# Holding the plan to late landings: a self-scheduling attention and SwiGLU kernel with new landing floors, fill products and load order

## The chip, the cores and the metric

The kernel runs on one core of one Trainium2 chip. The metric is the device time of that core in microseconds (us). The kernel before took 438.62 us, the median of five runs (436.72, 437.76, 438.62, 439.91 and 439.95). The profiled execution is the fastest of the five.

## The reference

The inputs are q, k and v of shape 8 x 12 x 448 x 64 (batch, heads, sequence, head width), two FFN weights of 768 x 1536, an output weight of 1536 x 768 and a norm gain of 768, all float32.

```python
scores = scale * np.matmul(q, k.transpose(0, 1, 3, 2))
attn = np.maximum(scores, 0.0) ** 2 / S
x = np.matmul(attn, v)            # heads are joined: 3584 tokens x 768
xn = x / np.sqrt(np.mean(x * x, axis=-1, keepdims=True) + 1e-06) * rms_g
g = xn @ w_gate
out = ((g * (1.0 / (1.0 + np.exp(-g)))) * (xn @ w_val)) @ w_out
```

So each batch goes through attention with a squared ReLU instead of a softmax, then RMS norm, a gated FFN and the output projection.

## The kernel before, in words

**Tiling.** Work goes by batch (448 tokens). For each pair of heads, scores are computed transposed (keys on the partitions) in units of two matmuls on the two row halves of the array, in tiles psS; the last 64 keys of two pairs share a unit psR. Each unit is rectified (`r`, L783 on VectorE or L785 on ScalarE) and squared (L791). The products with v (psAV) give xT, which is squared and summed over the features (psSS), turned into 1/rms, and scaled into xn. The FFN products psg and psv read xn and the weights; their product hT is read by the output products psO, whose copies `ost` are stored per tile of 128 tokens. Batch 0 is processed in two halves of 224 tokens (subs a0 and a1), the others whole.

**Transposes.** Scores need q and k with the head width on the partitions (tile qkT). Batches 0 and 1 are transposed by TensorE (psT, L645) and copied out. From batch 2 on, `transpose_dma` (L732) lets SyncE (SP) issue eight DMA transposes per batch, four from kb (k as loaded) and four from qb (q as loaded). They wait for the load. A score unit reads all 448 columns of q and so needs all four qb transposes of its batch.

**Queues.** All float32 loads are cast to bf16 on the way and are issued by GpSimd (POOL), in one order: k and q of batch 0, v of batch 0, then what the string ORDER names (weights by columns of 128, `w0-2` for wg and wv; `k` and `K` the first and second half of k and q of batch 1; `v` its v), then the two halves of wo, then k, q and v of batch 2, 3 and so on. A load is issued when the eighth load before it has landed. SP carries the DMA transposes and the stores of the output, in one order.

**The order is planned at build time.** Class Planner simulates TensorE's two row halves and the other engines. It has fixed costs for each instruction and a model of when each load lands (`issue`, with a rate and a lag). It picks, at each planned moment, the piece of work that is ready by that model: score units, transposes, products with v, FFN segments, output segments. The result is one fixed instruction stream for each engine; on the chip each engine takes its stream in order, and waits on real semaphores. So an instruction placed early in the stream of an engine holds up everything behind it until its own data are there. A score unit of a batch may be placed when its qkT is planned to be there and its turn (`due_of`) has come.

**Fill products.** Until the FFN has begun, where the plan sees TensorE without ready work for longer than a given time, `filler` and `fill` place matmuls of 128 x 224 into an unused bank (psB), to keep the array busy. Their planned cost is 189 ns before the planned time WARM and 96 ns after. They are ordinary instructions in TensorE's stream.

Of the kernel before, what the change touches and what calls it, by code (L numbers as in the profile page):

```python
# [14 lines left out]
U = 7  # L15
UH = 4
# [11 lines left out]
def latest(toks, at=0.0):  # L28
    for k in toks:
        if k.t is None:  # L30
            return None
        at = max(at, k.t)
    return at
# [21 lines left out]
class Planner:  # L55
# [1 line left out]


    SEM, PSUM, HAND, SW = 50.0, 210.0, 200.0, 95.0
    WARM = 5500.0  # L60
    either = ("square", "squared")
    SLACK = 0.0
    PEN = 0.0
    acts = ("relu",)

    def __init__(self, nc, tc, banks, wide, warm):
        self.nc, self.tc, self.banks, self.wide, self.warm = nc, tc, banks, wide, warm
        self.free = {"act": 1300.0, "dve": 1500.0, "pool": 750.0, "sp": 1300.0}
        self.tasks, self.seq = [], 0
        self.reserve = {e: 1e9 for e in self.free}  # L70
        self.t = [1100.0, 1100.0]
        self.mode = "row"
        self.ins = [[], []]
        self.aux = None
        self.cur, self.next0, self.q8 = None, [], []
        self.stream = []
        self.units, self.auxes, self.sneaks = [], [], []
        self.behind = mybir.DependencyInfo(
            mybir.DependencyClass.Sync, mybir.DependencyReason.DATA
        )  # L80
# [180 lines left out]
    def choose(self, t):  # L261
        self.auxes = [a for a in self.auxes if not a.void()]
        self.warm()
        for a in self.auxes:
            r = a.ready()
            if r is not None and r <= t:
                return t, lambda: self.set_aux(a)
        for a in self.sneaks:
            r = a.ready()
            if r is not None and r <= t:  # L270
                return t, lambda: self.sneak(a)
        s = self.stream_next(t)
        u = None
        if self.units and not any(a.holds() for a in self.auxes):
            u = self.units[0].ready()
        if u is not None and u <= t and (self.units[0].due() or s is None or s[0] > t):
            return t, self.begin_unit
        if s is not None and s[0] <= t:
            return t, lambda: self.slot(0, s[1])
        times = [s[0]] if s is not None else []  # L280
        if u is not None:
            times.append(u)
        for a in self.auxes + self.sneaks:
            r = a.ready()
            if r is not None:
                times.append(r)
        if self.warm() and (not times or min(times) > t + 250.0):
            return t, self.filler
        if not times:
            return None  # L290
        at = min(times)
        return at, lambda: self.skip(at)
# [47 lines left out]
def kernel(  # L340
# [24 lines left out]
    PE_T = 2  # L365
    R = 14
    PACE = 0.93
    GATE = 1
    LEAD = 3
    WIDE_T = 0  # L370
    DUE1 = 1
# [3 lines left out]
    HOLD = 900.0  # L375
    JOIN = 300.0
    LAG = 2800.0
    LASTW = (384, 192, 192)
    A2, A3, A5 = (384, 384), (256, 256, 256), (512, 256)
    W0 = (A2, A2, A3)  # L380
    WE = (A2, A2, A3)
    WO = (A2, A2, A2, A2)
    ORDER = "w0-2 w2-4 w4-6 k w6-8 w8-12 v K"
    FIRST = "k4-8 q8-12 k8-12 v0-4 v4-12 Q"
    AGATE = 6
    THIRD = 0
    THIRDV = 3
# [35 lines left out]

    ones_bf = const.tile([P, P], BF16, name="ones_bf", tag="ones_bf")
    nc.vector.memset(ones_bf[:], 1.0)
    busy_bf = const.tile([P, HALF], BF16, name="busy_bf", tag="busy_bf")
    nc.vector.memset(busy_bf[:], 0.0)
    eps_col = const.tile([P, 1], FP32, name="eps_col", tag="eps_col")
    nc.vector.memset(eps_col[:], eps)
    ident = const.tile([P, P], BF16, name="ident", tag="ident")  # L430
# [12 lines left out]
    def issue(fn, nbytes, run, need=(), rate=None, ahead=8):  # L443

        tok = Tok()
        land = dma["landed"]
        need = list(need) + (land[-ahead:][:1] if len(land) >= ahead else [])
        land.append(tok)
        rate = rate or (397.0 if run > 512 else 330.0)
        cost = 500.0 + 0.45 * nbytes / run  # L450

        def go(e):
            fn()
            end = pl.free["pool"]
            at = max(dma["t"], end + 900.0)
            dma["t"] = at + nbytes / (min(rate, 340.0) if 4600.0 < at < 9000.0 else rate)
            lag = 1750.0 if dma["t"] < 5000.0 else 1900.0 if dma["t"] < 6500.0 else LAG
            TRACE.append((end - cost, dma["t"] + lag - end + cost, "dma", "%d" % nbytes))
            return dma["t"] + lag - end

        pl.task(-1, {"pool": cost}, go, need, tok)
        return tok
# [45 lines left out]
        run = (u1 - u0) * D * 4  # L508
        landed(nm, b, h0, h1, issue(go, D * (h1 - h0) * run, run, need))

    def load_k0(h0, h1):

        if ("k", 0) not in ld:
            ld["k", 0] = fpool.tile([D, H, U * D], BF16, name="k0", tag="k0")
            ldtok["k", 0] = {}
        t = ld["k", 0]

        def go():
            nc.gpsimd.dma_start(
                out=t[:, h0:h1], in_=src_of["k"][0, h0:h1].rearrange("h (p u) d -> p h (u d)", p=D)  # L520
            )

        landed("k", 0, h0, h1, issue(go, S * (h1 - h0) * D * 4, U * D * 4))
# [65 lines left out]
    def wide_ready(n):  # L589
        f = sorted(x.free for x in wide if x.free is not None)  # L590
        return f[n - 1] if len(f) >= n else None
# [12 lines left out]
    def transposes(b, pairs, c0, c1, with_k, gate=lambda: True):  # L604

        done = Tok()
        for j in pairs:
            if with_k:
                kTok[b, j] = done
            for c in range(c0, c1):  # L610
                qTok[b, j, c] = done
        toks = [identTok]
        for j in pairs:
            for nm in ("k", "q") if with_k else ("q",):
                for hh in range(2):
                    lst = ldtok[nm, b][2 * j + hh]
                    if nm == "q" and b == 0:
                        lst = [lst[0]] if c0 == 0 else [lst[-1]]
                    toks += lst
        n = (c1 - c0) * PC  # L620
        width = (S if with_k else 0) + n * len(pairs)

        def ready():
            if not gate():
                return None
            r, f = latest(toks), bank_ready()
            return None if r is None or f is None else max(r, f)

        def run(s):
            bank = take_bank()  # L630
            ps = bank.take("psT", BF16, [P, 1024])
            t = new_qkT(b)
            steps = []
            end = s
            if with_k and b == 0:
                steps += [("k", pairs[0], u, D, u % UH * P + u // UH * D) for u in range(U)]
                end += pl.SW + U * (29.2 - 56.0)
            elif with_k:
                steps += [("k", pairs[0], c, P, c * P) for c in range(UH)]
            at = S if with_k else 0  # L640
            for i, j in enumerate(pairs):
                steps += [("q", j, c, PC, at + i * n + (c - c0) * PC) for c in range(c0, c1)]
            for nm, j, c, w, o in steps:
                for hh in range(2):
                    nc.tensor.transpose(  # L645
                        out=ps[hh * D : (hh + 1) * D, o : o + w],
                        in_=ld[nm, b][:w, 2 * j + hh, c * D : (c + 1) * D],
                        identity=ident[:w, :w],
                    )
            end += 56.0 * len(steps)  # L650

            def copy(e):
                if with_k:
                    dst = t[:, pairs[0]].rearrange("p t s -> p (t s)")[:, c0 * PC : c0 * PC + width]
                    src = ps[:, :width]
                else:
                    dst = t[:, pairs[0] : pairs[-1] + 1, 1, c0 * PC : c1 * PC]
                    src = ps[:, :width].rearrange("p (j s) -> p j s", s=n)
                if e == "dve":
                    copied[b, pairs[-1]] = nc.vector.tensor_copy(out=dst, in_=src)  # L660
                else:
                    copied[b, pairs[-1]] = nc.scalar.copy(out=dst, in_=src)

            pl.task(
                2, {"dve": dve_cost(width, 0.52), "act": act_cost(width)}, copy, [Tok(end + 200.0)],
                done, free_bank(bank),
            )
            return end

        pl.auxes.append(Aux("transposes", "col", ready, run))  # L670

# [690 lines left out]
        return sub.total - sum(1 for u in pl.units if u.sub is sub)  # L1362

    for j in range(HP):
        transposes(0, [j], 0, 2, True)
    pl.task(0, {"sp": 500.0}, load_g, [kTok[0, HP - 1]])
    for j in range(0, HP, 3):
        transposes(0, [j, j + 1, j + 2], 2, 4, False, gate=lambda: begun(a0) >= AGATE)
# [76 lines left out]
    def fill():  # L1445
# [4 lines left out]
        if bank.fill is None:  # L1450
            ps = bank.take("psB")
            bank.fill = ps[:, 0, :HALF] if bank in wide else ps[:, :HALF]
        nc.tensor.matmul(  # L1453
            out=bank.fill, lhsT=ones_bf[:], rhs=busy_bf[:], start=True, stop=True
        )
        cost = 96.0 if max(pl.t) > pl.WARM else 189.0
        bank.free = max(pl.t) + cost
# [46 lines left out]
```

## Time and profile before

| What | Value |
|---|---|
| median of five runs | 438.62 us |
| profiled execution, its own time | 436.72 us |
| its span in the profile | 434.9 us (1.8 us lie outside it) |
| TensorE (PE) busy | 428.9 us, 99% |
| VectorE (DVE), ScalarE (ACT) busy | 272.6 us (63%), 246.2 us (57%) |
| GpSimd (POOL) busy | 76.6 us, 18% |
| granted TensorE clock, mean | 0.998 |
| fill products | 71, of them 22 ahead of the first transpose |

Busy time of TensorE is a union of modelled spans, so 99% says that there is hardly a moment without a product, fill products included, not that the array is at its peak. The stretches between 0 and 25 us (start) and 80 and 125 us (batches 2 and 3 come in by DMA transposes) are those where something other than TensorE's own stream can set the pace.

### The profile page before, as it was taken

Reading aid. Unit: us, or ns where it says so; the run is one execution under the profiler, and the core shown is the slowest. Engines: PE = TensorE matmul, PEld = TensorE weight load, DVE = VectorE, ACT = ScalarE, POOL = GpSimd, SP = SyncE. Lnnn points to the kernel's source line nnn. Section 1 sums busy time; section 2 is a strip of 40 time slices with the busy share of each in tenths; the row PEclk is TensorE's granted clock in tenths of the full one; section 3 lists DMA queues with packets and bytes.
Section 4 is the critical chain, followed back from the end, with each engine's and each line's share of the span. In section 5 each row is a group of like instructions: output and inputs, shape, how many; then the busy total and the mean of one; then the engine's idle time right before and its main releaser. Section 6 shows DMA issues by size and latency. Waiting matters only on the chain.

```text
span 434.9 us, 12532 instructions
## 1 busy us (share of the span) xinstructions
PE 428.9 (99%) x5569; PEld 316.6 (73%) x5569; DVE 272.6 (63%) x445; ACT 246.2 (57%) x349; POOL 76.6 (18%) x95
## 2 busy tenths in 40 slices
PE   8999999999999999999999999999999999999996
PEld 6688788965579755884579855795569955699996
DVE  4888985458954776667854678577754677442200
ACT  5787774548553575747743576566744567342222
POOL 8442425401331320124012220100000000000000
PEclk9999999999999999999999999999999999999999
DMA  9999999999999992699949990672003200020023
GB/s 151 193 196 205 203 190 125 148 214 152 130 79 217 150 91 17 110 143 88 64 58 199 193 63 2 85 140 53 2 15 97 74 2 2 2 74 2 2 74 109
DMA packets 133237, 44.68 MB, mean 103 GB/s; under 512 B 104064, under 2 KB 129728, under 8 KB 133184
## 3 DMA queue, kind: packets, MB, share of 16 engines
q0 software_dynamic: 92880, 24.16, 57.2%
q1 hardware_dynamic: 39808, 19.50, 25.0%
q8 instruction: 43, 0.70, 0.7%
q10 hardware_dynamic: 496, 0.24, 0.2%
q14 instruction: 10, 0.08, 0.1%
HBM read 48.76 MB, written 11.01 MB: 137 GB/s over the span
## 4 chain that ended last, share of the span: by engine, by line
PE 90%; DMA 6%; SPq 2%; issue 1%; ACT 0%; DVE 0%; POOLq 0%
PE psg L146 24%; PE psv L146 24%; PE psO L146 23%; PE psAV L949 9%; PE psS L842 6%; DMA qb<-in_q_dram 3%; DMA qkT<-qb 2%; PE psT L645 2%; SPq L732 2%; PE psR L863 1%; DMA k<-in_k_dram 1%; PE psB L1453 1%; ACT r L785 0%; PE psSS L1130 0%; PE psSS L1054 0%
## 5 line engine op out<-in xcount | busy, mean ns | idle before, releaser
L146 PE MATMUL psv<-xn,wv_sb 64*128 64x448 bf16 (+1 forms) x1296 | 170.6, 329 | 0.0
L146 PE MATMUL psg<-xn,wg_sb 64*128 64x448 bf16 (+1 forms) x1296 | 170.6, 329 | 0.0
L146 PE MATMUL psO<-wo_sb,hT 64*128 64x384 bf16 (+2 forms) x1464 | 132.3, 310 | 0.0
L785 ACT ACTIVATE r<-psS 128x896 bf16<-128x896 f32 x121 | 108.4, 922 | 36.3 <-PE psS L842 35.5
L146 PEld LDWEIGHTS <-hT 64*128 64x128 bf16 x1464 | 109.8, 94 | 14.6 <-issue 2.5
L146 PEld LDWEIGHTS <-wv_sb 64*128 64x128 bf16 x1296 | 94.9, 94 | 31.3 <-issue 2.9
L146 PEld LDWEIGHTS <-wg_sb 64*128 64x128 bf16 x1296 | 95.5, 94 | 28.7 <-issue 2.5
L791 DVE TENSOR_TENSOR r<-r 128x896 bf16<-128x896 bf16 (+1 forms) x171 | 99.9, 613 | 10.4 <-ACT r L785 10.0
L1182 DVE TENSOR_TENSOR hT<-sil,psv 128x448 bf16<-128x448 bf16 x96 | 59.4, 619 | 56.0 <-PE psv L146 56.0
L1166 ACT ACTIVATE sil<-psg 128x448 bf16<-128x448 f32 x96 | 52.4, 546 | 49.0 <-PE psg L146 48.7
L842 PE MATMUL psS<-qkT 64*128 64x448 bf16 (+1 forms) x324 | 52.9, 329 | 0.1
L1260 ACT COPY ost<-psO 128x384 f32<-128x384 f32 (+2 forms) x51 | 23.1, 453 | 50.3 <-PE psO L146 50.1
L547 POOL DMA_DIRECT2D kb<-in_k_dram x42 | 31.7, 795 | 82.8 <-DMA qkT<-kb 63.1
L949 PE MATMUL psAV<-r,vb 64*64 64x448 bf16 (+1 forms) x756 | 43.4, 335 | 0.3
L980 DVE TENSOR_SCALAR xT<-psAV 128x896 bf16<-128x896 f32 (+1 forms) x22 | 22.2, 1007 | 28.6 <-PE psAV L949 28.6
L785 ACT ACTIVATE r<-psR 128x896 bf16<-128x896 f32 (+1 forms) x26 | 22.0, 847 | 31.5 <-PE psR L863 31.5
L783 DVE TENSOR_SCALAR r<-psS 128x896 bf16<-128x896 f32 x23 | 25.1, 1090 | 18.1 <-PE psS L842 17.9
L1104 DVE SCALAR_TENSOR_TENSOR xn<-xT,g_sb,rstd 128x448 bf16<-128x448 bf16 (+1 forms) x54 | 30.2, 629 | 7.9 <-ACT rstd L1088 7.8
L949 PEld LDWEIGHTS <-vb 64*64 64x64 bf16 x756 | 18.7, 105 | 20.1 <-PE psAV L949 7.9
L842 PEld LDWEIGHTS <-qkT 64*128 64x128 bf16 x324 | 19.9, 94 | 10.1 <-issue 1.3
L503 POOL DMA_DIRECT2D vb<-in_v_dram x18 | 13.7, 805 | 60.9 <-PE psO L146 40.5
L547 POOL DMA_DIRECT2D qb<-in_q_dram x6 | 13.7, 2275 | 40.5 <-DMA qkT<-qb 32.5
(49 smaller groups left out, 176.1 us busy)
## 6 DMA issues: line engine op xcount, KB each, us to landing
vb<-in_v_dram POOLq DMA_DIRECT2D x14, 384.0 KB, 11.4
kb<-in_k_dram POOLq DMA_DIRECT2D x42, 96.0 KB, 8.6
qb<-in_q_dram POOLq DMA_DIRECT2D x6, 672.0 KB, 9.1
out_dram<-ost SPq DMA_DIRECT2D x7, 336.0 KB, 3.4
wo_sb<-in_moe_w_out_dram POOLq DMA_DIRECT2D x2, 1152.0 KB, 21.5
out_dram<-ost SPq DMA_DIRECT2D x8, 288.0 KB, 2.8
out_dram<-ost SPq DMA_DIRECT2D x8, 240.0 KB, 3.9
wg_sb<-in_moe_w_gate_dram POOLq DMA_DIRECT2D x4, 384.0 KB, 12.8
```

The source lines that it names most:

```text
L146: mm = self.nc.tensor.matmul(out=seg.bank["tile"][:, off : off + seg.w], lhsT=lhsT[prt], rhs=rhs[prt], start=(seg.first and h == 0 and i = ...
L547: lambda o=o, i=i: nc.gpsimd.dma_start(out=o, in_=i),
L783: nc.vector.tensor_relu(out=r[:, :, :w], in_=ps[:, :, :w])
L785: nc.scalar.activation(out=r[:, :, :w], in_=ps[:, :, :w], func=ACT.Relu)
L791: nc.vector.tensor_tensor(out=r[:, :, :w], in0=r[:, :, :w], in1=r[:, :, :w], op=ALU.mult)
L842: nc.tensor.matmul(out=ps[:, hh, o : o + n], lhsT=t[prt, j, 0, c * P : (c + 1) * P], rhs=t[prt, j, 1, sub.q0 : sub.q0 + n], start=True, st ...
L949: mm = nc.tensor.matmul(out=ps[hh * D : (hh + 1) * D, jj, :n], lhsT=vt[prt, 2 * (ja + jj) + hh, u * D : (u + 1) * D], rhs=r[prt, hh, o : o ...
L980: nc.vector.tensor_scalar_mul(out=xT[at], in0=ps[:, :, :n], scalar1=inv_attn)
L1104: nc.vector.scalar_tensor_tensor(out=xn[:, kt, q0 : q0 + n], in0=xTs[b, 0][:, kt, q0 : q0 + n], scalar=g_sb[:, kt : kt + 1], in1=rstd[:, q ...
L1166: nc.scalar.activation(out=s[:, :m], in_=ps[:, :m], func=ACT.Silu)
L1182: nc.vector.tensor_tensor(out=h[:, fbs[0] : fbs[-1] + 1, o : o + n], in0=s[:, :m].rearrange("p (f s) -> p f s", s=n), in1=ps[:, :m].rearra ...
L1260: nc.scalar.copy(out=ost[:, c0 : c0 + w], in_=ps[:, :w])
```

## The change

- The landing model in `issue` gets a floor for each of the first eight loads: the planned landing is not earlier than the FLOOR entry (5850 to 14900 ns), which is the latest landing seen of that load. The early lag is 2050 instead of 1750 ns.
- Fill products read the constant tile of ones that the program always sets up, broadcast with a step of zero, instead of two tiles written by VectorE; `busy_bf` is gone. TensorE's plan begins at 700 instead of 1100 ns. WARM is 6500 instead of 5500 ns. A fill product may be placed for a planned gap of 110 instead of 250 ns.
- PEN: a rectification that could go to either engine is put to VectorE only if that is more than 200 ns earlier by the plan (before: 0). GATE: transposes of batch 1 may begin after two instead of one of a1's products with v.
- ORDER: the weights go in six pieces of 256 columns, with the halves of batch 1's k and q between them, and v of batch 1 last; wo follows as before.
- A transpose path in float32 (`transposes_f32`) is added but switched off (F32_T = 0).

```diff
-    WARM = 5500.0
+    WARM = 6500.0
+    GAP = 110.0
...
-    PEN = 0.0
+    PEN = 200.0
...
-        self.t = [1100.0, 1100.0]
+        self.t = [700.0, 700.0]
...
-        if self.warm() and (not times or min(times) > t + 250.0):
+        if self.warm() and (not times or min(times) > t + self.GAP):
...
-    GATE = 1
+    GATE = 2
...
     LAG = 2800.0
+    LAG0 = 2050.0
+    FLOOR = 5850.0, 8500.0, 9350.0, 10450.0, 11150.0, 11850.0, 13150.0, 14900.0
+    floors = []
...
-    ORDER = "w0-2 w2-4 w4-6 k w6-8 w8-12 v K"
+    ORDER = "w0-2 w2-4 k w4-6 w6-8 w8-10 K w10-12 v"
...
+    F32_T = 0
...
-    busy_bf = const.tile([P, HALF], BF16, name="busy_bf", tag="busy_bf")
-    nc.vector.memset(busy_bf[:], 0.0)
...
-            lag = 1750.0 if dma["t"] < 5000.0 else 1900.0 if dma["t"] < 6500.0 else LAG
-            TRACE.append((end - cost, dma["t"] + lag - end + cost, "dma", "%d" % nbytes))
-            return dma["t"] + lag - end
+            lag = LAG0 if dma["t"] < 5000.0 else 1900.0 if dma["t"] < 6500.0 else LAG
+            at = max(dma["t"] + lag, FLOOR[len(floors)] if len(floors) < len(FLOOR) else 0.0)
+            floors.append(at)
+            TRACE.append((end - cost, at - end + cost, "dma", "%d" % nbytes))
+            return at - end
...
     for j in range(HP):
-        transposes(0, [j], 0, 2, True)
+        if j < F32_T:
+            transposes_f32(j)
+        else:
+            transposes(0, [j], 0, 2, True)
...
         nc.tensor.matmul(
-            out=bank.fill, lhsT=ones_bf[:], rhs=busy_bf[:], start=True, stop=True
+            out=bank.fill,
+            lhsT=nc.const_aps.tensor(1.0, [P, P], BF16),
+            rhs=nc.const_aps.tensor(1.0, [P, HALF], BF16),
+            start=True,
+            stop=True,
         )
```

In the built instruction streams this gives 78 fill products instead of 71 (27 instead of 22 ahead of the first transpose), two POOL loads more, twelve rectifications of score units moved from VectorE to ScalarE, and these changes of place:

| In the stream | before | after |
|---|---|---|
| SP: the first two stores of the output | behind batch 2's four qb transposes | ahead of them, behind its four kb transposes |
| TensorE: psg (448 wide) ahead of the first read of batch 2's qkT | 43 | 53 |
| TensorE: psg, psv (448 wide) ahead of the first read of batch 3's qkT | 144, 144 | 139, 138 |
| TensorE: psO (384 wide), psAV (448 wide) ahead of it | 107, 156 | 96, 140 |
| TensorE: the first reader of batch 3's qkT | psR, between two halves of psAV | psS (four matmuls), ahead of the output segment |
| TensorE: what stands ahead of the first read of batch 4's qkT | | the same, fill products apart |

More of the change, by code (lines that the diff above doesn't have):

```diff
@@ L509, in load_runs, with new_k0 @@
         landed(nm, b, h0, h1, issue(go, D * (h1 - h0) * run, run, need))
-    def load_k0(h0, h1):
+    def new_k0():
         if ("k", 0) not in ld:
@@ L515, in load_k0 @@
             ldtok["k", 0] = {}
-        t = ld["k", 0]
+        return ld["k", 0]
+    def load_k0(h0, h1):
+        t = new_k0()
         def go():
@@ L668, in run, with transposes_f32, ready, over @@
             return end
+        pl.auxes.append(Aux("transposes", "col", ready, run))
+    def transposes_f32(j):
+        done = [Tok(), Tok()]
+        kTok[0, j] = done[0]
+        for c in range(2):
+            qTok[0, j, c] = done[1]
+        toks = [identTok]
+        for hh in range(2):
+            toks += ldtok["k", 0][2 * j + hh] + ldtok["q", 0][2 * j + hh][:1]
+        def ready():
+            r, f = latest(toks), wide_ready(1)
+            return None if r is None or f is None else max(r, f)
+        def run(s):
+            bank = take_wide()
+            ps = bank.take("psT")
+            t = new_qkT(0)
+            parts = (
+                ("k", [(u, D, u % UH * P + u // UH * D) for u in range(U)], S),
+                ("q", [(c, PC, c * PC) for c in range(2)], 2 * PC),
+            )
+            left = [2]
+            def over(t):
+                left[0] -= 1
+                if not left[0]:
+                    bank.free = t + 60.0
+            for i, (nm, steps, width) in enumerate(parts):
+                for c, w, o in steps:
+                    for hh in range(2):
+                        nc.tensor.matmul(
+                            out=ps[hh * D : (hh + 1) * D, i, o : o + w],
+                            lhsT=ld[nm, 0][:w, 2 * j + hh, c * D : (c + 1) * D],
+                            rhs=ident[:w, :w],
+                            start=True,
+                            stop=True,
+                        )
+                s += 2.0 * sum(w / 2.4 + 2.5 for _, w, _ in steps)
+                def copy(e, i=i, width=width):
+                    (nc.vector.tensor_copy if e == "dve" else nc.scalar.copy)(
+                        out=t[:, j, i, :width], in_=ps[:, i, :width]
+                    )
+                pl.task(
+                    2, {"dve": dve_cost(width), "act": act_cost(width)}, copy,
+                    [Tok(s + 200.0)], done[i], over,
+                )
+            return s + pl.SW
         pl.auxes.append(Aux("transposes", "col", ready, run))
@@ L1453, in fill @@
         nc.tensor.matmul(
-            out=bank.fill, lhsT=ones_bf[:], rhs=busy_bf[:], start=True, stop=True
+            out=bank.fill,
+            lhsT=nc.const_aps.tensor(1.0, [P, P], BF16),
+            rhs=nc.const_aps.tensor(1.0, [P, HALF], BF16),
+            start=True,
+            stop=True,
         )
```

## The prediction

> **What bounds the kernel now.** I read the page first: busy shares and the chain that ended last.
>
> ```profile
> span 434.9 us, 12532 instructions
> PE 428.9 (99%) x5569; PEld 316.6 (73%) x5569; DVE 272.6 (63%) x445; ACT 246.2 (57%) x349; POOL 76.6 (18%) x95
> ...
> PE 90%; DMA 6%; SPq 2%; issue 1%; ACT 0%; DVE 0%; POOLq 0%
> ```
>
> TensorE sets the end, but 8% of the chain runs over DMA and SP. Second, the waits of TensorE:
>
> ```profile
> PE psB L1453 <- DVE eps_col L429: 1.2, 1, 1.2
> PE psR L863 <- DMA qkT<-qb: 0.6, 1, 0.6
> PE psT L645 <- DMA k<-in_k_dram: 0.4, 1, 0.4
> PE psR L863 <- PE psAV L949: 0.2, 1, 0.2
> ```
>
> Two are at the start; two stand before psR, first readers of a batch's transposes. Third, the chain around them (start, length, what):
>
> ```profile
> 63.78 12.95 DMA qb<-in_q_dram
> 76.75 1.27 SPq L732
> ...
> 83.91 8.60 DMA qkT<-qb
> 92.51 0.29 issue
> 92.80 0.38 PE psR L863 x4
> ...
> 120.62 0.94 PE psAV L949 x16
> 121.56 0.14 issue
> 121.70 0.38 PE psR L863 x4
> ```
>
> Batch 2's gate opened at 92.80, after TensorE had stood still 0.60 us: the path to there is load of q, four transposes on SP, landing. At 121.70 there is a second one. The row names psAV, but at the two other places of this shape psR follows the sixteen psAV after 0.88 us (101.42 to 102.31, 110.46 to 111.34), so here it was free at 121.50 and began at 121.70. The DMA rows say why:
>
> ```profile
> 109.30 7.33 SPq L732 DMA_TRANSPOSE qkT<-qb  x4
> ...
> DMA to landing us min/median/max: 7.4/7.4/7.4
> ```
>
> The last of batch 3's four qb transposes was issued at 114.18 and landed 7.4 us later, at 121.6. So both batches come in just as TensorE wants them: whatever TensorE wins or loses before is taken up at these gates, and a gate that is reached earlier in the stream is a stall. Last, the timeline at the second gate:
>
> ```profile
> 118.57 0.32 PE L146 MATMUL psO<-wo_sb,hT 64*128 64x384 bf16 x1
> ...
> 120.55 0.95 PE L949 MATMUL psAV<-r,vb 64*64 64x448 bf16 x16
> ...
> 121.70 0.38 PE L863 MATMUL psR<-qkT 64*64 64x448 bf16 x4 [0.19 <-PE psAV L949]
> ```
>
> **The Trainium skill.** "TensorE: Matmul & The Clock Gate", Part 1: the array starts at half clock and is released after about 4 us of activity, by a free-running window. The trace agrees: 22 fill products took 4.26 us and stepped by 187 ns; the first 14 transposes took 0.58, the next 14 0.41. "DMA: Bandwidth & Descriptors", Issuing engines are not separate DMA queues: loads, transposes and stores share the same 16 engines; the page has DMA at 9 tenths or more in every slice up to 120 us. The same page, Anatomy of one DMA: the issuing sequencer does the waiting, not the DMA engine; so an unready store on SP holds what is queued behind it. No row of before shows a store ahead of the qb transposes.
>
> **The change part by part.** Times are against the profiled 436.72 us (span 434.9).
>
> Start: fill products need no VectorE any more. Other engines begin at 0.74, so they begin at 0.75 to 1.06 instead of 1.18; 27 x 0.187 = 5.05 us ends at 5.8 to 6.1; the first transpose, at 5.80 before, is 0 to 0.3 us later. A memset of 0.15 us leaves VectorE, idle there: nothing. A clock released at another moment changes the price of fill products, not what waits for data. Later fill products: 51 instead of 49, 2 x 0.096 = 0.2 us; one score unit (four products, some 0.3 us) more comes before the first FFN product. Sum for the start 0 to +0.5, less the 0.3 of work done earlier: about +0.1, from -0.3 to +0.5.
>
> Floors and lag: no instruction, only places. First landings were 5.76, 7.51, 8.56, 9.77, 10.44, 11.11, 12.50 and 14.19 in the profiled run; the floors are 0.1 to 1.0 later. Here they gain nothing; where loads land late, they spare stalls of up to about 1.0.
>
> Rectifications: twelve go from VectorE (1.09 us each) to ScalarE (0.92). No wait of TensorE names either engine beyond the memset; they hide behind TensorE, with 162 and 189 us idle; without that cover, 11 us on ScalarE.
>
> Loads: the same bytes in another order. Two more POOL issues, 0.84 each, behind landings that POOL waits for anyway. Batch 1's first k and q come before the third weight pieces: those move from 26.31 and 29.14 by the 0.74, 0.74 and 1.73 us of the k and q pieces, to 29.5 and 32.3; I estimate that the last, w10-12, lands at 45 and 47 instead of 40.15 and 44.05, against first uses at 44.04 and 46.91. Bound 0 to 0.9 us of stall; I take 0, as the plan has moved FFN work back too.
>
> SP: two stores now stand ahead of batch 2's qb transposes. They wait for both halves of the tile, copied at 75.27 and until 77.96; issuing them takes 0.52 and 0.45. So the transposes begin at 78.95 instead of 76.75: at most 2.2 us late. But kb transposes ahead of them were still landing until 84.47, so the queue does not run dry; what remains is the stores' own data, about 1.0 us a pair (pairs landed at 94.64, 95.76, 96.89). Bounds 0 and 2.2; I take 1.0: the gate opens at 93.8. Ahead of it stand 10 more psg (twelve take 1.13 us, from 85.04 to 86.17), 0.95 us, so TensorE arrives at 92.20 + 0.95 = 93.15, stalls 0.65, and the net is +0.05 (from -0.6 to +1.25).
>
> Batch 3's gate: now a psS ahead of the output segment. What stood before the gate and now stands behind it: 11 psg and psv, 11 psO (from 118.57 to 120.55, 1.98 us) and 16 psAV (0.88): 2.86 us. TensorE arrives at 118.57 plus the shifts above (-0.9 to +1.75; with late weights +2.65), so between 117.7 and 121.2, always before 121.6. So none of those shifts counts: the gate takes them up. The path to the gate is unchanged: q's load of batch 3, issued at 83.04 after the load before had landed (82.47), landed at 109.28; transposes 109.30 to 121.6; all bytes ahead are the same, only the two stores come sooner. I take 0, bounds -0.7 and +0.7 (how far I would trust my sums of landing steps). Behind the gate: 434.9 - 121.70 = 313.2 us as before, plus the 2.86. After it TensorE idled 0.1 us, so nothing absorbs this.
>
> Sum: 121.70 + 313.2 + 2.86 = 437.8 us of span, +1.8 outside it = 439.6, against 436.72: +2.9 us, 0.65%. On the median of 438.62: 441.5 us. That holds if the 1.9 us by which the median run exceeds the profiled one are in the DMA path (both kernels then wait for it).
>
> **Rivals.**
> - Not slower, the surplus was TensorE's: in the median run first loads land late and TensorE reaches batch 3 up to 1.9 us after its data. The new stream is then pinned at the gate, ending at 439.6: +1.0 us on 438.62, no change. For it: floors say that landings 1.0 later were seen. Against: a load path late at the start is late at the gate too.
> - Faster: batch 3's transposes land before TensorE arrives at 118.6, so over 3 us sooner. From there the stall is gone; it saves 0.6 + 0.2 of stalls, and in late runs up to 1.5 at the start: 436.4. For it: k and q pieces of batch 1 come 5 to 9 us sooner. Against: every byte ahead of batch 3's q is still ahead of it.
> - Slower still: the stores' wait delays the transposes by the full 2.2 us and this passes to batch 3's landing: 441.5 + 2.2 = 443.7. Against: batch 3's kb transposes waited for loads, until 92.07.
> - The change does nothing that it says: excluded for the places, which are in the built streams; if fill products from the constant ran at another pace, the gates would take it up.
>
> **How the numbers follow.** Likeliest case 0.58 (own range 440.4 to 442.6), surplus on TensorE 0.20, faster 0.12, slower still 0.10. Measurement tells about 0.5%, 2.2 us, from no change: faster is below 436.4, slower above 440.8. Most of the first case (0.51) and the last give slower 0.61; the rest of the first, the second and a little of the third give same 0.29; faster 0.10. The range leaves out most of the faster case and the top of the last: 438.1 to 443.4.
>
> **What would show it.** In the profile of after: a wait of TensorE for qkT<-qb of about 3 us before a psS near 118 to 122, as the longest wait; SP's stores at about 78 ahead of the qb transposes; the first gate at 93 to 95; idle of TensorE in 100 to 150 us of about 3 instead of 0.2 us. Wrong: no such wait, or batch 3's last landing before 119 or after 123.

## The result and the profile after

The changed kernel took 441.35 us in the median of 40 runs (437.76 to 449.86), the kernel before 438.67 us in 77 runs beside it (436.01 to 441.66). The ratio is 1.0051, 95% interval 1.0037 to 1.0065: slower by half a per cent. Ratios here, and the table by clock further down, leave out runs that lie over 1.5% above the fastest of their kernel (6 of 41 of after, none of before, 9 of 22 with the gate put back, at most 3 of any other); the medians quoted take all.

The profiled execution of after took 440.56 us, its span is 438.8. From its page, the span, the busy shares and the chain that ended last, by engine:

```profile
span 438.8 us, 12552 instructions
PE 430.2 (98%) x5576; PEld 317.1 (72%) x5576; DVE 263.3 (60%) x434; ACT 253.0 (58%) x359; POOL 78.3 (18%) x97
...
PE 91%; DMA 7%; SPq 1%; DVE 0%; issue 0%; ACT 0%
```

TensorE is busy 1.3 us longer than before (430.2 against 428.9) and the span is 3.9 us longer: most of the loss is time in which TensorE stands still. Its waits (in total, times, longest):

```profile
PE psR L925 <- DMA qkT<-qb: 2.3, 1, 2.3
PE psS L904 <- DMA qkT<-qb: 1.8, 1, 1.8
PE psB L1518 <- PEq L1557: 0.8, 1, 0.8
```

The stalls of 0.6 and 0.2 us before the first readers of batch 2's and batch 3's transposes are now 2.3 and 1.8, so the longest wait stands at batch 2's gate, not at batch 3's. ("Gate" is the first read of a batch's DMA transposes.) The wait for k at the start (0.4) is not in this list any more. The chain that ends at the second of them (start, length, what):

```profile
85.76 23.04 DMA qb<-in_q_dram
108.81 1.21 SPq L794
110.07 1.27 SPq L794
111.39 2.39 SPq L794
113.83 8.54 DMA qkT<-qb
122.37 0.09 issue
122.46 0.56 PE psS L904 x4
```

It is the path that the prediction named: load of q, four transposes on SP, landing. Before, it ended at 121.6 and TensorE came to it at 121.5; now it ends at 122.37, and TensorE had come at 120.69, as the timeline shows (in brackets: the idle time before):

```profile
122.46 0.56 PE L904 MATMUL psS<-qkT 64*128 64x448 bf16 x4 [1.77 <-DMA qkT<-qb]
```

Busy time of TensorE in two stretches, 90 to 100 and 100 to 150 us, after and then before:

```profile
90.00:100.00 10.00, 7.68 (x82) 5.20 (x80) 4.63 (x8) 4.07 (x7) 0.59 (x1) 1.00 1.82 185
100.00:150.00 50.00, 48.23 (x572) 34.52 (x570) 32.50 (x53) 31.79 (x46) 14.24 (x17) 1.00 1.60 148
```

```profile
90.00:100.00 10.00, 9.39 (x102) 5.62 (x99) 7.56 (x13) 6.43 (x9) 0.20 (x1) 1.00 1.70 220
100.00:150.00 50.00, 49.81 (x602) 35.36 (x600) 35.12 (x54) 28.13 (x41) 14.04 (x17) 1.00 1.45 147
```

The first figure behind the comma is TensorE's: 1.7 us less in one stretch, 1.6 less in the other; from 150 to 400 us it is 249.94 in both. Last, SP's timeline of after, and the copy on VectorE that the first stores wait for:

```profile
67.14 9.89 SPq L794 DMA_TRANSPOSE qkT<-kb  x4
78.47 0.83 SPq L1348 DMA_DIRECT2D out_dram<-ost  x2
79.39 9.32 SPq L794 DMA_TRANSPOSE qkT<-qb  x4
```

```profile
77.83 0.56 DVE L1324 COPY ost<-psO 128x384 f32<-128x384 f32 x1 [1.84 <-PE psO L147]
```

The two stores are ahead of the qb transposes, which begin at 79.39 instead of 76.75. Batch 2's q also landed later here, at 78.12 (before: 76.73), but that is not what set the time: the stores waited for the copy, which ended at 78.39, and the transposes followed them. So all of the 2.6 us are the stores' here. The last transpose landed at 95.76 instead of 92.51.

From the profile alone the sum is: the second gate opens 0.76 us later (122.46 against 121.70), and what follows takes 316.3 instead of 313.2 us, 3.1 more. Behind the gate TensorE is busy for 312.95 us, before for 309.91: 3.0 us of work have moved from before the gate to behind it. The 0.76 is less sure. In the 14 profiles of all kernels here, batch 3's last transpose landed between 119.95 and 125.58 us, and in that of after with three more products at the start, which has the same order of loads and transposes, at 123.36.

### The profile page after: what moved, and what is told of

The parts are those of the page before. It is cut to its first block, busy times and chain, and to the rows that moved or that the text cites. A ratio compares the mean times of both kernels' runs of the same rounds, so it can differ in the third digit from the quotient of the medians.

```text
span 438.8 us, 12552 instructions
## 1 busy us (share of the span) xinstructions
PE 430.2 (98%) x5576; PEld 317.1 (72%) x5576; DVE 263.3 (60%) x434; ACT 253.0 (58%) x359; POOL 78.3 (18%) x97
## 4 chain that ended last, share of the span: by engine, by line
PE 91%; DMA 7%; SPq 1%; DVE 0%; issue 0%; ACT 0%
PE psO L147 26%; PE psv L147 22%; PE psg L147 22%; PE psAV L1011 8%; PE psS L904 6%; DMA qb<-in_q_dram 5%; PE psB L1518 3%; DMA qkT<-qb 2%; PE psT L653 2%; SPq L794 1%; PE psR L925 1%; PE psSS L1192 0%; PE psSS L1116 0%; DVE qkT L668 0%; ACT ost L1322 0%
## 5 line engine op out<-in xcount | busy, mean ns | idle before, releaser
L847 ACT ACTIVATE r<-psS 128x896 bf16<-128x896 f32 x133 | 118.9, 921 | 33.2 <-PE psS L904 32.5
L847 ACT ACTIVATE r<-psR 128x896 bf16<-128x896 f32 (+1 forms) x25 | 21.1, 844 | 31.6 <-PE psR L925 31.6
L845 DVE TENSOR_SCALAR r<-psS 128x896 bf16<-128x896 f32 x11 | 12.0, 1089 | 14.9 <-PE psS L904 14.7
L1067 DVE TENSOR_TENSOR x2f<-xT 128x896 f32<-128x896 bf16 x18 | 19.5, 1086 | 2.0 <-ACT xT L1040 2.0
## 6 DMA issues: line engine op xcount, KB each, us to landing
qb<-in_q_dram POOLq DMA_DIRECT2D x6, 672.0 KB, 10.2
```

Source lines behind the costliest of these rows:

```text
L847: nc.scalar.activation(out=r[:, :, :w], in_=ps[:, :, :w], func=ACT.Relu)
L1067: nc.vector.tensor_tensor(out=got["x2"][:], in0=xT[at], in1=xT[at], op=ALU.mult)
```

## The experiments

Two questions: is the place of batch 3's first reader the cause, and what is the 1.9 us by which the median run of before exceeds its profiled one? Theory A, the prediction's: the early gate costs 2.9 us, and the surplus is in the DMA path, which both kernels wait for. Theory B, the prediction's first rival: the surplus is TensorE's at the start, and the gates of the changed kernel swallow it.

**The gate put back, all else as changed.** Batch 3's first psS waits in the plan until batch 3's first psR has been placed, so that this psR, behind the output products, is the first reader again:

```diff
-            if live["r"] >= R:
+            if live["r"] >= R or self.sub.b == 3 and not self.sub.ready_rest:
```

> The kernel after, with batch 3's first score unit held back until batch 3's psR, so that the first read of batch 3's transposes stands behind the same products as in the kernel before; SP's two early stores, batch 2's gate, fill products, floors and loads are those of after. Theory (the place of batch 3's gate sets the loss): the 2.86 us of products come back ahead of the gate, so about 438.5 us, ratio to before 0.997 to 1.003, and the wait for qkT<-qb before the psS of batch 3 (1.8 us in the profile of after) is gone. Rival 1 (SP's stores ahead of the transposes delay the loads and transposes up to batch 3): about 441.3, ratio 1.005, the gate opens late and the wait stands before psR instead. Rival 2 (the loss is in the start or in the moved rectifications): about 441.3 too, but with the wait gone.

Measured: 439.78 us, ratio 0.9990 [0.9966, 1.0014]. Its longest waits of TensorE:

```profile
PE psR L925 <- DMA qkT<-qb: 1.2, 1, 1.2
PE psB L1518 <- PEq L1557: 0.8, 1, 0.8
PE psT L653 <- DMA k<-in_k_dram: 0.6, 1, 0.6
```

The wait before psS is gone: TensorE is busy for 50.00 of the 50 us from 100 to 150, and behind the gate for 309.99, as in the kernel before. So is the loss, with every other part of the change in place, in the eleven runs at full clock (a mean of 0.998 or more): they took 437.37 to 438.48. But ten of the 22 runs have a mean clock of 0.985 or less and took 443.93 to 450.92, so that the mean of all 22, 441.96, is no lower than that of after (441.65). The experiments on the start, below, bear on these ten.

**The early gate alone, in the kernel before.**

```diff
-        if not sub.pace:
+        if not sub.pace or sub.b == 3 and i == 0:
```

> The kernel before, with one thing changed: batch 3's first score unit is due at once, which places its psS ahead of 34 FFN products, 11 psO and 16 psAV that stood before the gate (34 x 0.0945 + 11 x 0.081 + 0.88 = 5.0 us). Theory: all of it is lost: about 443.5 us, ratio 1.010 to 1.012, with a wait for qkT<-qb of up to 5 us before that psS at about 121.6. Rivals 1 and 2: no change of SP, start or rectifications, so 438.7, ratio 1.000.

Measured: 442.97 us, ratio 1.0064 [1.0039, 1.0089]. From the timeline of TensorE (what stands in brackets is the idle time before):

```profile
122.41 0.56 PE L842 MATMUL psS<-qkT 64*128 64x448 bf16 x2 [4.40 <-DMA qkT<-qb]
122.73 2.07 PE L146 MATMUL psg<-xn,wg_sb 64*128 64x448 bf16 x9
```

The direction is right, the size was overrated: a stall of 4.4 us in one profile gives a ratio of 0.6% (by the medians 4.1 us, 0.9%), not 1.0 to 1.2%. Part of the stall may take up time by which the start of the median run is late: a hint at B, no more. And the products behind the stall are slow. Nine psg take 2.07 us, where twelve take 1.40 in the same view of before, at 85.04 us: the clock is at half from 121.65 to 125.06 us.

**Both gates late, in the kernel before and in the changed one.** The planned landing of batch 2's transposes is put off by 6 us, that of batch 3's by 4, so that their readers come later in the stream:

```diff
-                return 8000.0
+                return 8000.0 + {2: 6000.0, 3: 4000.0}.get(b, 0.0)
```

> The kernel before, with the planned landing of batch 2's DMA transposes 6 us and of batch 3's 4 us later, so that both gates stand later in TensorE's stream (batch 2's behind 64 more FFN products, batch 3's behind 44 more psO). Theory: TensorE no longer waits for qkT<-qb; the 0.6 + 0.2 us of the profiled run come back, and in the median run what it waits beyond that, up to 1.9: 436.0 to 437.9, ratio 0.994 to 0.998. If the surplus of the median run lies in the start and not in the DMA path, only 0.8 comes back: 437.9. Rivals 1 and 2 say no change, 438.7.

> The kernel after, with the same later planned landings of batches 2 and 3 (batch 2's gate behind 74 more FFN products than in before, batch 3's behind 48 more psO). Theory: no wait for qkT<-qb, and the start of after then shows unmasked: equal to the kernel before with late gates, or up to 1 us below it where first loads land late: 435.5 to 437.5, ratio to before 0.993 to 0.997. Rival 2 (the new start or the moved rectifications cost time): 2 to 3 us above the kernel before with late gates. Rival 1: no change against after, 441.3.

Measured: before with late gates 439.92 us, ratio 1.0020 [1.0003, 1.0036], a miss; after with late gates 437.97 us, ratio 0.9994 [0.9970, 1.0017], somewhat above its expectation. In neither does TensorE wait for qkT<-qb. So in the old kernel nothing is gained where the stalls of 0.6 and 0.2 us go away. Its start may explain part of that: its clock was released only at 13.6 us in the profile (before: 6.3), and a TensorE that comes late finds no stall to save. Why it is even 0.2% slower stays open. In the changed kernel 3.4 us are gained, and with late gates the changed kernel takes 2.0 us less than the old one. That speaks for B, though the two differ in loads and rectifications too, not in the start alone.

**The new fill taken out, and put in alone.** The first is the changed kernel with late gates and the old fill settings; the second the old kernel with the fill edits, gates untouched; the third this with late gates (batch 2's by the 6 us above, batch 3's by holding its units back until half of batch 2's products with v are placed). The edit of the first, against the changed kernel with late gates:

```diff
-    WARM = 6500.0
-    GAP = 110.0
+    WARM = 5500.0
+    GAP = 250.0
...
-        self.t = [700.0, 700.0]
+        self.t = [1100.0, 1100.0]
```

> The changed kernel with both gates late (as the run that took 437.97 us) and the start's fill products as they were: 64 instead of some 80, begun only as far as the old plan asks. If the start of the new fill is what makes that run 2 us faster than the old kernel with late gates (439.92), this one goes back to about 439.5 to 440, ratio 1.001 to 1.003 to the kernel before, and its granted TensorE clock is below 1 for longer in the first 15 us. If the fill is worth nothing (my prediction took -0.3 to +0.5 us for the start), it stays at 437.9, ratio 0.999.

> The kernel before with the fill edits alone (constant tile, fills planned to the old planned work). Gates where they were. If the surplus of the median run of before over its profiled run lies in a late release of TensorE's clock at the start and the longer fill ends it: 437 to 437.5 us, ratio 0.996 to 0.998. If the surplus lies in the transfers, or the gates absorb the earlier start: 438.7, ratio 1.000.

> The kernel before with the fill edits and with both gates some 3 to 5 us of work later. If the fill's gain is real and was masked by the gates: 436 to 437 us, ratio 0.994 to 0.998, no wait of TensorE for the transposes of q. If the fill is worth nothing: as the old kernel with late gates, 439.9, ratio 1.002.

Measured: 440.94 us, ratio 1.0031 [1.0011, 1.0051]; 440.56 us, 1.0030 [1.0009, 1.0051]; 441.24 us, 1.0042 [1.0019, 1.0064]. The first came in above its expectation, with the long spell at half clock; the other two are misses in sign. The same fill settings help in one kernel and hurt in another, so what counts is not the settings as such. The stretches of the first one show what it is (TensorE's busy time, number of products, granted clock):

```profile
4.90:8.30 3.40, 2.15 (x46) 1.00 1.30 206
8.30:18.50 10.20, 10.04 (x134) 0.50 1.51 192
```

The 25 products ended at 5.3, k landed at 6.5. The clock had been released at 4.89; 3.41 us later it was halved, for 10.2 us. In the old kernel with the new fill, the release came at 3.79, the rest of the 25 products then ran in half the time and ended at 4.8; k landed at 6.3; the clock was halved at 7.2. Products placed by count cover less time the sooner the clock is released: 25 took 4.54 us in the first of these profiles and 4.03 in the second. In the changed kernel, which plans k's landing later, they are 27.

**Four, and three, more products at the start.** The first is the kernel whose stretches stand above, with 29 instead of 25 products; then late gates with 30 instead of 27; the changed kernel with 30 instead of 27; the old one with 25 instead of 22. They are placed without a planned cost, so that nothing else in the streams has a reason to move. The edit of the first:

```diff
+    more = [4]
...
+        for _ in range(1 + (more.pop() if more else 0)):
```

> The changed kernel with late gates and the old fill (the run that took 440.94 us, where TensorE waited 1.25 us for the first k, its clock was granted for 3.4 us, was halved for 10.2 us, and 19 of 22 runs had a mean clock of 0.988 or less), with four more products at the start, 25 to 29, and nothing else. Theory (an idle stretch of over some 0.9 us in the first window of 3.41 us after the clock's release halves the clock again): the wait for k shrinks to about 0.5 us, at most 7 of 22 runs have a mean clock below 0.99, and the median falls to 437 to 438 us, ratio 0.994 to 0.997. If instead the late fills between products of use are what keep the clock, the runs stay at 440.5 to 441.

> The changed kernel with late gates and the new fill (437.97 us; 8 of 22 runs at a mean clock below 0.99, 4 us or more longer than the others), with three more products at the start, 27 to 30. Theory as above: the runs with a low clock vanish nearly, and the three products cost nothing where k lands at 6.2 and up to 0.5 us where it lands at 5.8: median 437.5 to 438.2, ratio 0.995 to 0.998, highest run below 441. If the low clock has another cause, a third of the runs stay above 441.

> The changed kernel itself with three more products at the start. The gates stay where they are, so the loss stays: 440.5 to 441.5 us, ratio 1.003 to 1.006; runs with a mean clock of 0.985 or less vanish. If the runs at a clock of 0.995 come from the stalls at the gates (1.7 us for a half clock of 3.4 us) they stay, about a third of all; if they come from the start they vanish, and the median falls to 440.

> The kernel before with three more products at the start, 22 to 25, and nothing else. 20 of its 54 fast runs had a mean clock of 0.988 and a span of 438.4 us, against 436.0 (0.996) and 437.1 (1.000). Theory: those at 0.988 vanish, median 437.8 to 438.5, ratio 0.997 to 0.999, all of the difference in the share of runs. If the fill was long enough already: 1.000 or, with 0.3 us of later start, 1.001.

The first: 437.45 us, ratio 0.9964 [0.9946, 0.9983], instead of 440.94 and 1.0031; 20 of 22 runs have a mean clock of 0.998 or more, without the four products 5 of 22 (16, not the 19 of the expectation, were at 0.988 or less). Its stretches, to be laid beside the two above:

```profile
4.90:8.30 3.40, 3.31 (x54) 1.00 1.26 197
8.30:18.50 10.20, 10.12 (x227) 1.00 1.57 192
```

227 products instead of 134 in the same 10.2 us. In this profile k also landed earlier than in the other (5.7 against 6.5 us) and the clock was released later (5.38 against 4.89), so it is the count of runs that settles the start, not the pair of profiles: the gap before the first transposes cost the kernel without the four products about 3 us (0.67% by the ratios, each to the kernel before beside it; 3.5 us by the medians).

The second: 437.95 us, ratio 0.9998 [0.9971, 1.0025]; the median as expected, the ratio not, since 3 of 14 runs still had a low clock, the highest at 443.27. The fourth, the old kernel: 437.65 us, ratio 0.9971 [0.9954, 0.9989]; its runs at a mean clock under 0.99 fall from 23 of 67 to 1 of 22. So the surplus of before's median run was in good part TensorE's, at the start: B. The expectation put all of the gain in the share of such runs; the table below shows that those at 0.998 and more gain too, by 2.3 us. An earlier release of the clock, which the mean doesn't show, would do that; no profile of such a run was taken. The one that was taken is of a run at 0.992: the clock was released at 4.04, the 25 products ended at 5.11, k landed at 6.75, and from 7.45 to 14.28 the clock was at half. Three more are not always enough.

Put together, with all runs counted: of the versions of the changed kernel with 27 products at the start, 30 of 99 runs have a mean clock under 0.99; of those with 29 or 30 products, 5 of 58.

The third, the changed kernel, stays slow: 442.60 us, 1.0062 [1.0040, 1.0083], above its expectation; and 11 of 20 runs have a mean clock around 0.996. Its profile caught why. First a wait, then two stretches at batch 3's gate:

```profile
PE psS L904 <- DMA qkT<-qb: 2.7, 1, 2.7
```

```profile
121.00:124.40 3.40, 0.94 (x11) 1.00 0.71 65
124.40:127.80 3.40, 3.40 (x22) 0.50 0.13 12
```

After a stall of 2.7 us the clock is halved for 3.4 us: 22 products where the stretch of the same length behind the gate of the profiled run of after, 122.59 to 126.00, holds 46. That is 1.7 us on top of the stall. TensorE came to this gate at 120.74 us here and at 120.69 in the profiled run of after; the span is 441.4 against 438.8, 2.6 us more: 0.9 from the longer stall, the rest, 1.7, is about what the half clock costs.

**The stores behind the transposes, in the changed kernel.** SP's order as before; the planner then puts batch 3's gate back by itself.

```diff
-            pl.task(0, {"sp": 800.0}, send, [tok] if tail else osts[key][1])
+            behind = [kTok[2, 0]] if (i, t) == (0, 0) else []
+            pl.task(0, {"sp": 800.0}, send, ([tok] if tail else osts[key][1]) + behind)
```

> The changed kernel with the first tile's stores planned behind batch 2's transposes on SP, as before the change; the planner then puts batch 3's first read back to its old place. To be compared with the run that only puts that read back (439.78, ratio 0.999; gate 2's stall 1.2 us). My prediction priced the stores ahead of the transposes at +0.05 us net (-0.6 to +1.25): if so, ratio 0.998 to 1.000 here and a stall at batch 2's gate of 0 to 1 us. A rival in which the order on SP makes the loss would give clearly less than the other run, 438.5 or below.

Measured: 438.58 us, ratio 0.9992 [0.9966, 1.0019]; against the first experiment (0.9990) there is no difference. From SP's timeline, from the timeline of TensorE, and from SP's timeline of the first experiment:

```profile
78.18 8.56 SPq L794 DMA_TRANSPOSE qkT<-qb  x4
86.85 2.04 SPq L1348 DMA_DIRECT2D out_dram<-ost  x4
```

```profile
94.38 0.38 PE L925 MATMUL psR<-qkT 64*64 64x448 bf16 x4 [1.35 <-DMA qkT<-qb]
```

```profile
78.91 0.87 SPq L1348 DMA_DIRECT2D out_dram<-ost  x2
79.87 8.74 SPq L794 DMA_TRANSPOSE qkT<-qb  x4
```

The transposes still begin at 78.18, not at 76.75, since SP waits there for the load of q; and batch 2's gate opens at 94.38, against 95.18 in the first experiment, with the stores ahead. In that run q had landed already at 75.51, and the transposes began at 79.87, behind the stores: the order alone held them back by more than 4 us. So by these profiles the order on SP is worth 0.8 us or more at this gate, depending on when q lands, and nothing at the end. The stall of 1.4 is above the 0 to 1 that I had expected.

**Runs by their mean clock** (number, median us). The mean is taken from the first release, so a late release doesn't lower it (with the release at 13.6 us it still was 0.999): runs at 0.998 and more can be long, and those of before are longer than its runs around 0.996. 3.4 us at half clock lower the mean by 0.004, 10.2 us by 0.012.

| Kernel | 0.998 and more | 0.993 to 0.997 | below |
|---|---|---|---|
| before, all comparisons | 64, 438.85 | 44, 437.78 | 81, 440.11 |
| before, three more products | 9, 436.56 | 9, 437.77 | 4, 439.34 |
| after | 19, 440.01 | 13, 441.99 | 3, 442.89 |
| after, three more products | 8, 439.81 | 11, 442.95 | 1, 443.94 |
| after, gate back | 11, 437.93 | 1, 441.08 | 1, 443.93 |
| after, gates late | 14, 437.89 | 1, 437.69 | 4, 441.86 |
| after, gates late, old fill, four more | 20, 437.39 | none | 2, 441.50 |

Among the versions of the changed kernel, runs around 0.996 are frequent only where batch 3's gate is early: 24 of 55, against 2 of 54 in the last three rows (with the runs of the transposes first and of late gates with 30 products, 4 of 79). In the old kernel they are frequent too; the one profile of such a run, with the new fill and late gates, has the half clock at the start, from 9.25 to 12.66 us. At full clock the early gate costs 2.1 us (440.01 against 437.93). And it brings spread: after's 19 runs at full clock lie between 437.76 and 441.73, the eleven with the gate put back within 1.1 us. A gate that TensorE waits at would hand on the spread of its landing.

## Why the prediction was right, and where it was not

441.5 us was forecast, 441.35 measured, and the main step held. The way to the number has two errors that cancel: the surplus of 1.9 us was not carried over (at full clock after is 1.2 us above before, not 2.9), and half clocks, which no step had, made up most of the rest. That forecast and result lie 0.15 us apart is luck.

- **Batch 3's gate, moved work: right.** 2.86 us forecast, 3.0 of busy time and 3.1 of span in the profile; putting the reader back takes the loss away, though it is 2.1 us in runs at full clock. "None of the shifts before it counts" held too: TensorE came to batch 2's gate at 93.57 (forecast 93.15; the 0.4 were there earlier, the copy before the stores ended 0.43 later too), left it at 95.89, 3.1 later than before, and with 0.95 of psg done ahead it came to batch 3's at 120.69, within the 117.7 to 121.2 given. The gate took it up.
- **The longest wait, forecast at about 3 us before a psS: 1.8, and not the longest.** Batch 2's gate, with 2.3, had taken the rest.
- **Batch 2's gate, stores ahead of the transposes: mis-sized.** Forecast +1.0, at most 2.2, a stall of 0.65. The transposes began 2.6 late (2.2 forecast), landed 3.25 late, and TensorE stood still for 2.3. The term that failed is the 1.0 of these 2.2: I held that the queue would not run dry, and that only the stores' own data would delay the landing. But the transposes' delay reached their landing whole. In all 14 profiles batch 2's last transpose landed 15.2 to 17.4 us after the first was issued, whether that was at 75.42 or at 82.99. None of it reached the end.
- **"The path to the gate is unchanged", ±0.7 for batch 3: 0.76.** q of batch 3 landed 0.5 sooner (108.79), and the transposes still ended later. The bounds were too narrow for what differs from run to run: from the first of the four to the last landing it took 12.2 to 15.4 us, and q itself landed between 106.16 and 113.05.
- **Floors, "they gain nothing" here: right for the profiled run, but they are no latest landings.** In 10 of the 14 profiles the first k landed after the floor of 5.85, up to 6.75, and the products at the start had ended before.
- **Start, +0.1 (-0.3 to +0.5): right for the profiled run** (27 products as counted, the first transpose at 5.91), **and wrong as a description.** "A clock released at another moment changes the price of fill products, not what waits for data" is the step that failed. The products' end, set against the landing of k, decides whether the clock is halved again, for 3.4 to 10.2 us.
- **"If the 1.9 us surplus of the median run is in the DMA path": wrong.** Three products at the start take 1.2 us off the old kernel's median, so much of the surplus is TensorE's. The first rival had this, though not the reason: it had late landings alone, not the clock. Its sum, +1.0 us, is what the runs of after at full clock show: 440.01 against 438.85, +1.2. But 13 of 35 runs lie 2.0 us above these. No step of the prediction had that: that a stall before a gate can be paid twice, once as a stall and once as a half clock after it. For the runs of after themselves this is inferred from their mean clock, and from its rarity in the versions of the changed kernel without the early gate; seen directly it is in two other kernels.
- **The faster and the still slower rival** did not come about in the profiled run: the last landing was neither before 119 nor after 123.

Left open are the two kernels that stay slower than their gates and clocks explain: the old one with late gates, and the old one with new fill and late gates (439.34 at full clock, from 3 runs). Open, too, is why a clock under 0.99 is as frequent as 10 of 22 with the gate put back and 8 of 41 in after, with the same 27 products at the start. The parts of the change that I took at zero (rectifications, weight pieces) were not tried alone; in no profile of after does TensorE wait for weights.

Two versions beat both kernels: the changed one with late gates, the old fill and four more products (0.9964), and the old one with three more products (0.9971).

## What to carry to other kernels

Where a fixed instruction stream meets data from a long DMA path, look for the place of the first reader: here, what moved from before that reader to behind it was paid (3.0 us of work, 2.1 to 3.1 us of time) since the data were the later of the two, and shifts ahead of it cost nothing at the end. Fill products should be planned to last beyond the latest landing by time, not by count, since an early release of the clock shortens the time that a count covers (25 products: 4.54 or 4.03 us). When the median run is longer than the profiled one, look at the granted clock of each run before deciding which engine the difference belongs to.

## What the runs showed of the hardware

- The Trainium skill, "TensorE: Matmul & The Clock Gate", Part 1, has the clock fall back after an idle window of about 3.4 us. Here a window of 3.41 us with much work in it was enough. Busy time of TensorE in the first window after the release, by profile: 2.67, 2.75, 2.77, 2.85, 3.10, 3.33 and three times 3.41 us, and the clock stayed; 1.72, 1.84, 2.16, 2.28 and 2.35 us, and it was halved in the next. So if busy time is what counts, the bound at the start, where products are small, lies between 69% and 78% in these 14 profiles.
- It is no bound on busy time as such: at batch 3's gate, with windows of 3.41 us counted on from the release, one of 1.64 us of busy time (profiled run of after, 119.18 to 122.59, products of 448 columns) kept the clock, one of 0.97 (the run with 30 products) and one of 0 us (the early gate in the old kernel) lost it. What is counted was not settled.
- The spells at half clock after the release lasted 3.41, 6.83 or 10.24 us, one to three windows. The release itself came between 3.8 and 13.6 us after the span's start.
- DMA transposes of batches 2 and 3, the four of q in a row on SP, landed 7.1 to 9.9 us after the last was issued, in all 14 profiles.
